# Last block of an attention and bilinear-GLU kernel: weight sums kept in DRAM, down products of two pairs at once, weight parts in a ring

## The chip, the cores and the metric

The kernel runs on one core of a Trainium2 chip. The metric is the device time in microseconds from the first to the last instruction of one execution. Three runs of the kernel before gave 2437.68, 2438.53 and 2443.07 us; the median is 2438.53 us. Engines are named as in the profile: PE is TensorE (PEld its weight loads), DVE VectorE, ACT ScalarE, POOL GpSimd, SP the engine that issues nearly all DMAs here.

## What is computed

The reference is a transformer block in float32 over 2048 rows of width 576. First comes attention with 32 query heads of 18 and one shared key and value head; then a bilinear GLU with 4608 hidden columns:

```python
h  = x + attention(layernorm(x))              # wq, wk, wv, wo
xn = layernorm(h)
h2 = h + ((xn @ w_gate) * (xn @ w_up)) @ w_down
```

The change touches only the second part, the products with w_gate, w_up and w_down.

## The kernel before

**Blocks and row blocks.** The 2048 rows are worked in four blocks of 512 (NB = 4, numbered 0 to 3). Hidden columns come in 36 groups of 128 (`f`); two neighbouring groups are a pair (NC = 18 pairs). Matmuls take float32 data in a faster 32-bit format, so that every operand is split into a high part (a copy, mostly on ACT) and a low part (operand minus high part, on DVE), and every product is made of three: high by high, high by low, low by high.

**Blocks 0 to 2** run in `ffn` (L905). Each step of the `f` loop, called a row block in the prediction, makes gate and up for 128 hidden columns with 27 double matmuls (L927, index `j` from 0 to 26 in the loop). In between stand the attention matmuls of later blocks (`pair`, L606 and L611, with their exponentials on ACT at L607), the split of the next weights (`split_w`, L808: high part on POOL at L92, low part on DVE at L93), and auxiliary work. After every second row block `down` (L843) makes the down product of the pair before.

**`down`** uses a seven-product scheme (Strassen-Winograd) on 2 x 2 blocks. The left operands are seven combinations of quarters of the hidden activations, in the tile `room` (A); the right operands are seven combinations of w_down, made at the start of the kernel and kept in DRAM (`wd_dram`), from which they come back through a ring of ten tiles (`wdo`, WD_BUFS = 10, `load_wd`). The product runs in 14 stages (`STAGES`, L1448): three matmuls of 128x288 into one of three PSUM banks, then an eviction which adds the bank to the residual `h`. Eight of the 14 evictions are one DVE instruction (L888); six are a copy on ACT (L892) and an add on POOL (L893).

**Block 3** runs in `last_block` (L1105). There attention is over, and gate and up too use the seven-product scheme, on quarters of the 512 input columns and rows. `ahead` (L977) prepares the activations during the last row blocks of block 2, a step at a time (the tables AHEAD and TURNS say at which `f` and `j`). The last 64 of the 576 input columns are added as a tail. For each pair, in this order, PE makes products 1, 2 (tail), 5, 6, 3 (tail), 7 (tail), 4 (tail), twelve matmuls of 128x256 each and four a tail (L1123, L1129). They go into two PSUM tiles: `s0`, whose two halves serve alternate pairs, and `s1`. Between products PE makes two, four or more stages of the down product of the pair before (`go`).

What follows a product, in each engine's own order of issue: copies of the PSUM banks to SBUF on ACT (c1, c5, c2), three adds on DVE (L1190 gu11, L1206 gu12, L1212 gu22), gate times up on POOL for three quarters of the hidden tile (`both_halves`, L1132: a11, a21, a22) and on DVE for the last (L1233 copies half of product 4's bank, L1234 multiplies: a12). The sums S of the quarters and their high and low parts (L92, L93) make the left operands A of the down product.

The weights of a pair are prepared while the pair before runs, in `prepare` (L1049): four loads of 256 KB and the tail weights, four POOL sums (L1074, L1081, L1087, L1093), seven high parts on ACT (L1058) and seven low parts on DVE (L1064), and both parts of the tail weights (L1060, L1066). Two full sets of seven weight tiles are held: one in freed tiles (`wrs`, `room`, `wps`, `wss`), one in the tile `XW`.

**Order.** The schedule is written out by hand: each engine works its instructions in the order in which the Python code issues them, and waits by semaphore for tiles that other engines write or free.

Of the kernel before, what the change touches and what calls it, by code (L numbers as in the profile page):

```python
# [26 lines left out]
P = 128  # L27
# [30 lines left out]
class Block:  # L58
# [846 lines left out]
    def ffn(self, b):  # L905
        pe, act, dve = self.pe, self.act, self.dve
        X, hid, todo = self.X, [], None
        ahead = self.ahead()
        for f in range(NF):
# [12 lines left out]
            for c in range(9):  # L922
                for wk, xk in ((0, 0), (0, 1), (1, 0)):
# [48 lines left out]
        self.load_wd(self.n_wd + 4)  # L972
# [4 lines left out]
    def ahead(self):  # L977
# [6 lines left out]
        for s in range(NQ):  # L984
            dve.tensor_scalar(xh[:, s, 0:D], h[:, s, :], mv[:, s, 0:1], rs[:, s:s + 1], ALU.subtract, ALU.mult)
            pool.tensor_copy(xh[:, s, D:], xh[:, s, 512:D])
            if s % 2:
                yield
# [10 lines left out]
        names = (1, 2, 5, 6, 3, 7, 4)  # L999
        self.XS = XS = {}  # L1000
        for i, k in enumerate(names[:5]):
            pl, tag = (self.pp, "P") if i < P_BUFS - 2 else (self.p2, "P2")
            XS[k] = pl.tile([P, 4, HT], F32R, tag=tag, name=f"XS{k}")
        XS[7], XS[4] = (self.kT[:, i * 4 * HT:(i + 1) * 4 * HT].rearrange("p (n q) -> p n q", n=4) for i in range(2))
        part = lambda i, j: raws[i][:, :, j * HT:(j + 1) * HT]
        sums = self.op.tile([P, 9, HT], F32, tag="ob", name="xsums")
        low = {k: sums[:, 2 * i:2 * i + 2] for i, k in enumerate((5, 6, 4, 7))}
        diff = sums[:, 8]
# [5 lines left out]
        dve.tensor_tensor(low[7], b22, b12, ALU.subtract)  # L1014
        yield
        src = {**low, 1: b11, 2: b21, 3: b22}
        for k in names:
            act.copy(XS[k][:, 0:2], src[k])
            dve.tensor_tensor(XS[k][:, 2:4], src[k], f32(XS[k][:, 0:2]), ALU.subtract)
            yield  # L1020
        xt = self.qp.tile([P, 4, HT], F32R, tag="q", name="XT_t")
        xd = self.qp.tile([P, 4, HT], F32R, tag="q", name="XT_d")
        rt = rt.rearrange("p (j q) -> p j q", j=2)
        act.copy(xt[:, 0:2], rt)
        dve.tensor_tensor(diff, rt[:, 0], rt[:, 1], ALU.subtract)
        dve.tensor_tensor(xt[:, 2:4], rt, f32(xt[:, 0:2]), ALU.subtract)
        act.copy(xd[:, 0], diff)
        dve.tensor_tensor(xd[:, 1], diff, f32(xd[:, 0]), ALU.subtract)
        self.Xt = [(xt[:, 0], xt[:, 2]), (xt[:, 1], xt[:, 3]), (xd[:, 0], xd[:, 1])]
        del rt, src, low, b11, b12, b21, b22, xt, xd, sums, diff, raws, part  # L1030
        yield
        raw = self.op.tile([P, 5, TB], F32, tag="ob", name="raw")
        self.raw = {k: raw[:, i] for k, i in ((1, 0), (6, 0), (2, 1), (3, 1), (5, 2), (4, 3), (7, 4))}
        self.wt_raw = self.wp.tile([P, 2, 2, P], F32, tag="wor", bufs=1, name="wt_raw")
        prep = self.prepare(0)
        next(prep)
        next(prep)
        yield
        sets = [self.wp.tile([P, 4 * HT], F32R, tag="wr", bufs=2, name=f"wrs{i}") for i in range(2)]
        sets += [self.o_hl.rearrange("p k q -> p (k q)")]  # L1040
        sets += [self.pp.tile([P, 4 * HT], F32R, tag="P", name=f"wps{i}") for i in range(2)]
        wss = self.wp.tile([P, 2, 4 * HT], F32R, tag="ws", bufs=2, name="wss")
        sets += [wss[:, 0], wss[:, 1]]
        as_set = lambda x: x.rearrange("p (l c g m) -> p l c g m", l=2, c=2, g=2)
        self.WS = [{k: as_set(x) for k, x in zip(names, sets)}, None]
        self.Wt = self.wp.tile([P, 2, 2, 2, P], F32R, tag="wos", bufs=1, name="wt")
        yield from prep

    def prepare(self, m):  # L1049

        act, dve, pool, sp = self.act, self.dve, self.nc.gpsimd, self.sp
        n = m % 2
        raw = self.raw
# [523 lines left out]
```

## Time and profile before

| | us |
|---|---|
| median of three runs | 2438.53 |
| the profiled execution's own time | 2437.47 |
| its span in the trace | 2435.7 |
| first row block of block 0 | from 377 |
| output of block 0 written from | 928 |
| output of block 1 written from | 1477 |
| first product of block 3 | 1963.3 |
| first product of pair 1 | 1992.6 |

The profiled execution's time is 1.8 us longer than its span. Busy shares of the span: PE 95%, PEld 68%, DVE 53%, ACT 63%, POOL 32%. The mean granted TensorE clock is 0.975 of full speed.

How to read the rows that the prediction shows: a row of the view by stage gives the window, its length, then for each engine the busy time and the number of instructions, the granted clock, the mean share of the DMA engines and their rate. A row of waits names who waited for whom, the total in us, how many times, and the longest. A row in order of time gives the start, the time from the first start to the last end, the engine and line, and in brackets the idle time ahead of it and what ended it; matmuls are pipelined, so that two rows overlap and their spacing is read from start to start. A row of groups gives the form, the count, busy us and mean ns of one, then the idle time ahead.

### The profile page before, as it was taken

The numbers are of one execution on the slowest core, as the hardware profiler recorded it, in microseconds if no ns is written. First come the engines' busy times: TensorE is split into PE (matmuls) and PEld (weight loads), VectorE is DVE, ScalarE is ACT, GpSimd is POOL, SyncE is SP. The second block draws the span as 40 slices with busy tenths as digits, with TensorE's granted clock in tenths as the row PEclk, the third lists the DMA queues.
The fourth block names the chain that finished last, engine by engine and source line by source line (L and its number), as shares of the span: only waits on it lengthen the run. The fifth ranks groups of instructions, "written<-read, shape, count | busy, mean of one in ns | idle before, by whom it ended". The sixth has DMA issues, their size and how long they took to land.

```text
span 2435.7 us, 46083 instructions
## 1 busy us (share of the span) xinstructions
PE 2304.3 (95%) x17958; PEld 1667.6 (68%) x17958; DVE 1291.1 (53%) x2238; ACT 1528.7 (63%) x2095; POOL 782.7 (32%) x892
## 2 busy tenths in 40 slices
PE   7999999999999999999999999999999987887887
PEld 5333346777777777777777777777777887877877
DVE  7556553434343454444444454444447677677675
ACT  6888877676767666676767675767662343344442
POOL 5345301222222222222222222222222355565563
PEclk9999999999999999999999999999999998888888
DMA  5788734333333336333333345334334444444442
GB/s 173 255 262 287 266 101 146 122 115 123 116 123 116 124 108 195 115 125 116 125 114 121 109 132 159 125 114 126 113 119 147 165 141 139 126 130 145 122 136 80
DMA packets 165428, 345.68 MB, mean 142 GB/s; under 512 B 17581, under 2 KB 49197, under 8 KB 165205
## 3 DMA queue, kind: packets, MB, share of 16 engines
q1 hardware_dynamic: 162469, 331.42, 42.7%
q0 software_dynamic: 2736, 11.26, 1.5%
q8 instruction: 143, 2.34, 0.4%
q14 instruction: 80, 0.66, 0.1%
HBM read 274.80 MB, written 55.67 MB: 136 GB/s over the span
## 4 chain that ended last, share of the span: by engine, by line
PE 71%; DVE 10%; ACT 3%; issue 3%; POOL 1%; DMA 1%; SPq 0%; DVEq 0%; ACTq 0%; POOLq 0%
PE pg L927 19%; PE acc L611 14%; PE y L882 14%; PE s L606 9%; PE pu L927 5%; PE gs L1123 5%; PE yo L736 2%; DVE XW L1064 2%; PE gu L927 1%; ACT room L92 1%; DVE h L888 1%; DVE room L93 1%; DVE wps L1064 1%; DVE S L1215 1%; PE y L855 1%
## 5 line engine op out<-in xcount | busy, mean ns | idle before, releaser
L607 ACT ACTIVATE P<-s 128x1024 f32<-128x1024 f32 x1024 | 1026.2, 1027 | 280.5 <-PE s L606 201.3
L927 PE MATMUL pu<-X,ws 64*128 64x512 f32 x2565 | 693.4, 389 | 0.0
L927 PE MATMUL pg<-X,ws 64*128 64x512 f32 x2565 | 692.9, 389 | 0.0
L893 POOL TENSOR_TENSOR h<-h,tmp 128x288 f32<-128x288 f32 x408 | 342.5, 863 | 802.5 <-ACT tmp L892 801.7
L927 PEld LDWEIGHTS pg<-X,ws 64*128 64x128 f32 x2565 | 475.3, 185 | 66.7 <-DMA wdo<-wd_dram 0.8
L611 PE MATMUL acc<-P,V 128*32 128x512 f32 x4096 | 490.2, 598 | 0.7 <-ACT P L607 0.6
L927 PEld LDWEIGHTS pu<-X,ws 64*128 64x128 f32 x2565 | 472.6, 185 | 16.4
L882 PE MATMUL y<-wdo,room 128*128 128x288 f32 x2856 | 429.3, 304 | 38.2 <-DVE h L888 38.2
L882 PEld LDWEIGHTS y<-wdo,room 128*128 128x128 f32 x2856 | 399.3, 193 | 84.1 <-DVE h L888 43.3
L606 PE MATMUL s<-q,kT 56*128 56x512 f32 x2048 | 437.9, 422 | 6.5 <-ACT P L607 3.9
L888 DVE TENSOR_TENSOR h<-h,y 128x288 f32<-128x288 f32 x544 | 235.1, 451 | 243.0 <-PE y L882 241.9
L892 ACT COPY tmp<-y 128x288 f32<-128x288 f32 x408 | 161.6, 402 | 302.3 <-PE y L882 298.6
L606 PEld LDWEIGHTS s<-q,kT 56*128 56x128 f32 x2048 | 196.8, 184 | 207.3 <-ACT P L607 120.4
L611 PEld LDWEIGHTS acc<-P,V 128*32 128x32 f32 x4096 | 114.4, 109 | 246.8 <-issue 234.5
L92 POOL CAST ws<-wr 128x1152 fp32r<-128x1152 f32 x108 | 126.6, 1173 | 382.2 <-PE pu L927 224.8
L955 DVE TENSOR_TENSOR hf<-pu,g 128x512 f32<-128x512 f32 x95 | 65.7, 692 | 340.9 <-ACT g L951 340.9
L93 DVE TENSOR_TENSOR ws<-wr,ws 128x1152 fp32r<-128x1152 f32 x108 | 148.9, 1379 | 60.8 <-POOL ws L92 60.8
L93 DVE TENSOR_TENSOR room<-S,room 128x1024 fp32r<-128x1024 f32 (+1 forms) x85 | 86.1, 1012 | 157.3 <-ACT room L92 156.8
L1123 PE MATMUL gs<-XS,XW 128*128 128x256 f32 x540 | 84.5, 313 | 33.6 <-DVE hfl L1234 33.2
L1123 PEld LDWEIGHTS gs<-XS,XW 128*128 128x128 f32 x540 | 77.9, 216 | 37.7 <-DVE hfl L1234 35.1
L92 ACT CAST room<-S 128x1024 fp32r<-128x1024 f32 (+1 forms) x85 | 74.0, 871 | 37.4 <-DVE S L1226 30.9
L1132 POOL TENSOR_TENSOR hfl<-gu 128x256 f32<-128x256 f32 x36 | 26.9, 747 | 185.8 <-DVE gu L1190 184.7
(241 smaller groups left out, 2454.5 us busy)
## 6 DMA issues: line engine op xcount, KB each, us to landing
wdo<-wd_dram SPq DMA_DIRECT2D x492, 288.0 KB
wr<-in_wgu_dram SPq DMA_DIRECT2D x108, 576.0 KB
wd_dram<-wd_room SPq DMA_DIRECT2D x20, 1008.0 KB
raw<-in_wgs_dram SPq DMA_DIRECT2D x72, 256.0 KB
q<-q_dram SPq DMA_DIRECT2D x64, 216.0 KB
q_dram<-qs SPq DMA_DIRECT2D x16, 504.0 KB
wd_dram<-wd_hi SPq DMA_DIRECT2D x7, 1008.0 KB
wd_dram<-wd_src SPq DMA_DIRECT2D x7, 1008.0 KB
```

The source lines that it names most:

```text
L92: (copy or self.cast)(hi, src)
L93: self.dve.tensor_tensor(lo, src, f32(hi), ALU.subtract)
L606: self.pe.matmul(s_[:, i], self.kT[o:o + 56, t * P:(t + 1) * P], q[o:o + 56, pr], start=True, stop=True)
L607: self.act.activation(p_, s_, AF.Exp, scale=SCALE)
L611: self.pe.matmul(acc[32 * j:32 * j + 32, :], self.V[:, t, :], Ps[j // 2][:, j % 2, :], start=(t == 0), stop=(t == NT - 1), skip_group_chec ...
L882: pe.matmul(y[:, :HD], m[:, t * P:(t + 1) * P], k, start=(first and j == 0), stop=(j == 2), skip_group_check=True)
L888: dve.tensor_tensor(hs, hs, y[:, :HD], ALU.add)
L892: act.copy(z, y[:, :HD])
L893: pool.tensor_tensor(hs, hs, z, ALU.add)
L927: pe.matmul(ps, w[o:o + 64, wk, c], X[o:o + 64, xk, c], start=(j == 0), stop=(j == 26))
L1064: dve.tensor_tensor(half(k, 1), raw[k], f32(half(k, 0)), ALU.subtract)
L1123: pe.matmul(bank[:, g * HT:(g + 1) * HT], W[:, wk, c, g], X[:, 2 * xk + c], start=(first and g == c == wk == xk == 0), stop=(c == 1 and wk ...
```

## The change

It has three parts.

1. **Weight sums in DRAM.** A new generator `weight_sums` makes the four sums of each of the 18 pairs on POOL during blocks 0 and 1, in two tiles that it takes from the `wdo` ring, and stores them in `wsum_dram`. One step (load, add, store) is taken at j = 8, 16 and 24 of each `f`. With two of the ten tiles held, the down weights are loaded eight ahead there (`load_wd(WD_BUFS - 2)`), and two more at the end of block 1.
2. **Down for two pairs.** In block 3, `down_pairs` makes the down product of pairs p - 2 and p - 1 together while pairs p and p + 1 run: 14 stages of six matmuls over four PSUM banks, three of each pair into the same bank, and one eviction for both. Four of the 14 evictions (ASIDE) go by ACT and POOL, ten by DVE. A has three copies in turn (AB), two of them in `XW`. Pair 16 goes alone behind the loop, then pair 17's plain products.
3. **Weight parts in a ring.** `prepare` goes. `feed(i)`, called behind each product i, makes the low part for product i + 2 (DVE), the high part for i + 3 (ACT) and the load for i + 7 (SP; of a plain weight for three products of seven, of a stored sum for four) in a ring of seven weight tiles and five raw ones.

Beside these the left operands' high and low parts are issued apart (`high`, `low`) instead of together, and `ahead` is cut into other steps with new tables.

```diff
+        if b == 0:
+            self.sums = self.weight_sums()
+            next(self.sums)
...
+                    if b < 2 and j in (8, 16, 24):
+                        next(self.sums, None)
...
-        self.load_wd(self.n_wd + 4)
+        self.load_wd(self.n_wd + (6 if b == 1 else 4))
...
+    def feed(self, i):
+        act, dve, sp = self.act, self.dve, self.sp
+        n = i + 2
+        if 0 <= n < 7 * NC:
+            w = self.WS[n % 7]
+            dve.tensor_tensor(w[:, 1], self.raw[:, n % 5], f32(w[:, 0]), ALU.subtract)
+        n = i + 3
+        if 0 <= n < 7 * NC:
+            act.copy(self.WS[n % 7][:, 0], self.raw[:, n % 5])
+        n = i + LEAD
+        if 0 <= n < 7 * NC:
+            m, k = divmod(n, 7)
+            sp.dma_start(self.raw[:, n % 5], self.wgs[m, :, (0, 1, None, None, None, None, 2)[k]] if k in (0, 1, 6) else self.wsum_dram[m, :, k - 2])
...
+    def weight_sums(self):
+        pool, sp = self.nc.gpsimd, self.sp
+        u, v = (self.wp.tile([P, TB], F32, tag="wdo", bufs=WD_BUFS, name=f"wsum{i}") for i in range(2))
+        for m in range(NC):
+            for k, (loads, to, x, y, op) in enumerate((([(u, 3), (v, 2)], u, u, v, ALU.add), ([(v, 0)], u, u, v, ALU.subtract),
+                                                       ([(v, 1)], v, v, u, ALU.subtract), ([(u, 0), (v, 3)], u, u, v, ALU.subtract))):
+                for t, j in loads:
+                    sp.dma_start(t, self.wgs[m, :, j])
+                yield
+                pool.tensor_tensor(to, x, y, op)
+                yield
+                sp.dma_start(self.wsum_dram[m, :, k], to)
+                yield
+
+    def down_pairs(self, b, pairs):
+        banks = [self.ps_f(f"yq{pairs[0]}_0"), self.ps_f(f"yq{pairs[0]}_1"), self.ps_m(f"yq{pairs[0]}_2"), self.ps_a(f"yq{pairs[0]}_3")]
+        for i, (bank, (x, w), first, (s, n)) in enumerate(QUAD):
+            W = [self.wdo.pop((b, p, w)) for p in pairs]
+            for t in range(2):
+                y = banks[2 * bank + t]
+                for z, (p, v) in enumerate(zip(pairs, W)):
+                    A = self.AB[(p + 1) % 3]
+                    for j, (k, l) in enumerate(((0, 0), (0, 1), (1, 0))):
+                        pe.matmul(y[:, :HD], A[:, k, x, t * P:(t + 1) * P], v[:, l], start=(first and z == j == 0),
...
+                if 2 * i + t not in ASIDE:
+                    dve.tensor_tensor(hs, hs, y[:, :HD], ALU.add)
+                else:
...
+                    act.copy(z, y[:, :HD])
+                    pool.tensor_tensor(hs, hs, z, ALU.add)
+                if t:
+                    del W, v
+                    self.load_wd(self.n_wd + len(pairs))
+                yield
```

The new order behind product 7 of a pair (`i + 5`), up to the next pair's product 1:

```diff
+            product(i + 5, a)
+            tail(1, 1, a)
+            dve.tensor_tensor(gu22, a, c5, ALU.add)
+            both_halves(a22, gu22)
...
+                dve.tensor_tensor(S[:, 2], a11, a21, ALU.subtract)
+                high(5, S[:, 2])
+            go(2)
...
+            self.feed(i + 5)
+
+            product(i + 6, a)
+            tail(1, 2, a)
...
+                low(5, S[:, 2])
                 dve.tensor_tensor(S[:, 0], a21, a22, ALU.add)
+                high(2, a22)
                 dve.tensor_tensor(S[:, 1], S[:, 0], a11, ALU.subtract)
+                go()
+                high(3, S[:, 0:2], 2)
+                low(2, a22)
             g = self.hh.tile([P, TB], F32, tag="g", bufs=1, name=f"gl{p}")
             act.copy(g[:, 0:HT], a[:, 0:HT])
+            if not end:
+                low(3, S[:, 0:2], 2)
             dve.tensor_tensor(a12, a[:, HT:], g[:, 0:HT], ALU.mult)
```

In the changed file gu22 is L1207, S[:, 2] L1213, the DVE eviction L1108, the weight low part L1058, the left operands' low part L1157, S[:, 0] and S[:, 1] L1230 and L1232, a12 L1240.

More of the change, by code (lines that the diff above doesn't have):

```diff
@@ L1029, in ahead @@
+        for i in range(len(todo) + 1):
+            if i < len(todo):
+                act.copy(todo[i][0], todo[i][2])
+            if i:
+                hi, lo, x = todo[i - 1]
+                dve.tensor_tensor(lo, x, f32(hi), ALU.subtract)
+            yield
         self.Xt = [(xt[:, 0], xt[:, 2]), (xt[:, 1], xt[:, 3]), (xd[:, 0], xd[:, 1])]
[L1030 to L1032 removed]
@@ L1033, in ahead @@
-        self.raw = {k: raw[:, i] for k, i in ((1, 0), (6, 0), (2, 1), (3, 1), (5, 2), (4, 3), (7, 4))}
+        del rt, src, low, b11, b12, b21, b22, xt, xd, sums, diff, raws, part, todo, hi, lo, x
+        self.raw = self.op.tile([P, 5, TB], F32, tag="ob", name="raw")
         self.wt_raw = self.wp.tile([P, 2, 2, P], F32, tag="wor", bufs=1, name="wt_raw")
[L1035 to L1039, printed above, removed]
```

294 lines of the change are left out of this document (126 added, 168 removed).

## The prediction

> **What bounds the kernel now.** I read the page's slices first, then busy time by stage, PE's waits, PE's order of time inside the last block, and the granted clock in short windows.
>
> ```profile
> span 2435.7 us, 46083 instructions
> PE   7999999999999999999999999999999987887887
> DVE  7556553434343454444444454444447677677675
> PEclk9999999999999999999999999999999998888888
> 930.00:1476.00 546.00, 545.24 (x4499) 394.51 (x4496) 252.97 (x453) 373.55 (x482) 128.87 (x151) 1.00 0.40 127
> 1600.00:1963.00 363.00, 354.09 (x2866) 270.39 (x2864) 194.93 (x358) 198.31 (x288) 102.40 (x120) 0.99 0.41 130
> 1992.60:2436.00 443.40, 355.57 (x2462) 342.56 (x2462) 302.10 (x492) 175.56 (x384) 241.12 (x217) 0.87 0.42 128
> ```
>
> The stage rows give PE, PEld, DVE, ACT, POOL, granted clock, DMA share, GB/s. Up to 1963 us (blocks 0 to 2) PE is hardly idle and its clock is full: 0.8 us of 546 are free in block 1, 9 of 363 at the end of block 2. In the last block (1963 to 2436) PE loads weights 342.6 us of 443.4 and the clock falls to 0.87. Only there is time to be won.
>
> ```profile
> PE gs L1123 <- DVE hfl L1234: 55.1, 17, 4.0
> PE y L882 <- DVE h L888: 30.4, 18, 1.9
> 2412.60 1.59 PE L1123 MATMUL gs<-XS,XW 128*128 128x256 f32 x12
> 2414.03 0.95 PE L882 MATMUL y<-wdo,room 128*128 128x288 f32 x6
> 2414.82 1.60 PE L1123 MATMUL gs<-XS,XW 128*128 128x256 f32 x12
> 2416.26 0.64 PE L1129 MATMUL gs<-XT_t,wt 128*128 128x256 f32 x4
> 2416.74 0.95 PE L882 MATMUL y<-wdo,room 128*128 128x288 f32 x6
> 2424.62 0.64 PE L1129 MATMUL gs<-XT_d,wt 128*128 128x256 f32 x4
> 2431.00 0.65 PE L1156 MATMUL gs<-wdo,room 128*128 128x288 f32 x3 [0.55 <-DVE h L1170]
> 1932.77 5.94 PE L882 MATMUL y<-wdo,room 128*128 128x288 f32 x33 [3.50 <-DVE h L888]
> 1963.33 1.70 PE L1123 MATMUL gs<-XS,wrs 128*128 128x256 f32 x12
> 1968.67 0.53 PE L855 MATMUL y<-wdo,room 128*128 128x288 f32 x2 [3.25 <-ACT room L92]
> 1992.60 0.62 PE L1123 MATMUL gs<-XS,XW 128*128 128x256 f32 x3 [3.99 <-DVE hfl L1234]
> ```
>
> Two waits carry it: product 1 of the next pair waits for DVE's product at L1234 (both lie in the tile s0; 3.24 us a pair), and a stage of the down product waits until DVE has emptied its bank (30.4/17 = 1.8). The last pair, with no weights to prepare, shows undisturbed PE by start-to-start times: 12 matmuls of a product 1.43 us, six of a down stage 0.79, a tail of four 0.48. A pair is 7 x 1.43 + 4 x 0.48 + 42/6 x 0.79 = **17.46 us** of PE. It takes (2425.1 - 1992.6)/17 = 25.4. PEld is idle 443.4 - 342.6 = 100.8 us, about 6 of it behind the last matmuls, so 5.6 a pair; the remaining 2.4 is the lowered clock. The fault is DVE's queue, 302.1/17 = 17.8 us of work a pair in an order that PE waits for.
>
> **The clock**, in windows as long as its own steps:
>
> ```profile
> 2215.50:2218.91 3.41, 1.59 (x12) 1.36 (x12) 2.98 (x7) 1.02 (x3) 3.41 (x4) 1.00 0.54 172
> 2218.91:2222.32 3.41, 2.56 (x13) 2.27 (x11) 3.18 (x6) 1.61 (x4) 1.54 (x2) 0.50 0.67 200
> 2222.32:2225.74 3.42, 1.71 (x8) 1.71 (x9) 2.98 (x6) 1.42 (x4) 0.00 (x0) 0.50 0.82 258
> 2242.80:2246.22 3.42, 2.32 (x19) 2.32 (x19) 3.02 (x6) 1.45 (x3) 3.42 (x4) 1.00 0.54 177
> 2246.22:2249.63 3.41, 0.24 (x2) 0.03 (x1) 2.81 (x5) 1.10 (x2) 0.32 (x1) 1.00 0.86 250
> 2249.63:2253.04 3.41, 2.91 (x13) 2.91 (x14) 2.32 (x6) 0.81 (x2) 0.00 (x0) 0.50 0.52 198
> 2253.04:2256.46 3.42, 3.42 (x29) 3.34 (x27) 1.39 (x3) 0.74 (x2) 0.00 (x0) 1.00 0.32 86
> 2010.70:2014.11 3.41, 1.77 (x14) 1.67 (x14) 3.02 (x7) 0.91 (x2) 3.41 (x4) 1.00 0.44 164
> 2014.11:2017.52 3.41, 0.89 (x8) 0.68 (x6) 2.82 (x6) 1.61 (x4) 0.96 (x1) 1.00 0.81 250
> ```
>
> The clock changes at the ends of fixed 3.41 us windows. After 1.36 us of weight loads in a window it halves; after 1.67 or 2.32 it does not. At half it returns after 2.91, not after 2.27. So an idle stretch of some 1.9 us inside one window costs a window at half clock, about 1.65 us of matmuls.
>
> **The change, part by part**, with these rows:
>
> ```profile
> L1064 DVE TENSOR_TENSOR XW<-raw,XW 128x512 fp32r<-128x512 f32 x57 | 60.1, 1076 | 0.2
> L93 DVE TENSOR_TENSOR room<-hf,room 128x512 fp32r<-128x512 f32 x19 | 13.0, 685 | 0.7 <-ACT room L92 0.7
> L888 DVE TENSOR_TENSOR h<-h,y 128x288 f32<-128x288 f32 x136 | 59.1, 448 | 39.1 <-PE y L882 38.3
> L1212 DVE TENSOR_TENSOR gu<-gs,cs 128x512 f32<-128x512 f32 x17 | 11.5, 678 | 1.4 <-PE gs L1129 1.4
> L1066 DVE TENSOR_TENSOR wt<-wt_raw,wt 64x512 fp32r<-64x512 f32 x16 | 11.7, 732 | 10.6 <-ACT wt L1060 10.6
> L93 DVE TENSOR_TENSOR room<-S,room 128x256 fp32r<-128x256 f32 x17 | 7.2, 425 | 0.6
> L1234 DVE TENSOR_TENSOR hfl<-gs,gl 128x256 f32<-128x256 f32 x18 | 7.5, 418 | 3.1 <-ACT gl L1233 3.1
> L1087 POOL TENSOR_TENSOR raw<-raw 128x512 f32<-128x512 f32 x16 | 27.9, 1741 | 0.0
> L1074 POOL TENSOR_TENSOR raw<-raw 128x512 f32<-128x512 f32 x16 | 20.7, 1292 | 0.0
> L1132 POOL TENSOR_TENSOR hfl<-gu 128x256 f32<-128x256 f32 x34 | 25.2, 741 | 183.4 <-DVE gu L1190 182.3 <-DVE gu L1212 1.1
> DMA packets 30276, 59.63 MB, mean 126 GB/s; under 512 B 3360, under 2 KB 3360, under 8 KB 30240
> GB/s 173 255 262 287 266 101 146 122 115 123 116 123 116 124 108 195 115 125 116 125 114 121 109 132 159 125 114 126 113 119 147 165 141 139 126 130 145 122 136 80
> ```
>
> *Sums moved.* 72 POOL adds of 1.29 to 1.74 us leave block 3 for blocks 0 and 1, with 108 loads and 72 stores of 256 KB on SP's queue. The steps stand a third of a row block apart (546/36/3 = 5.1 us): load, add, store. Cover: POOL works 129 us of 546 there, DVE 253, and no add stands ahead of the weight cast of the same row block. An add that waits for its load holds POOL's eviction adds and the next weight cast, and through that DVE; a load that waits for the store before it holds SP's loads of down weights, queries and heads. All of these are wanted several us later. Between 0 (nothing is removed there, so no gain) and 72 x 1.74 = 125 us I take 2, nearer PE's 0.8 us of idle time. The down ring keeps eight places of ten; seven are wanted every second row block, 30 us: nothing.
>
> *Weight parts in block 3.* Seven low parts a pair stay on DVE, at 1.08 us beside POOL's sums, 0.69 without them (the 685 ns row of the same size): -2.7 us a pair. Three more loads a pair: 15 transfers are 7 x 288 + 8 x 256 KB = 4.2 MB, at 21.4 us 195 GB/s against a mean of 126 now and 287 in the page's fourth slice: nothing, while each raw load has four products (9 us) to land.
>
> *Down for two pairs.* 14 evictions for 28: DVE's five a pair instead of eight (-1.3 us), POOL's two for six. A stage is six matmuls over four banks, so the 1.8 us bank wait goes. DVE a pair: 7 x 0.69 + 0.73 + 3 x 0.68 + 5 x 0.45 + 9 x 0.43 + 0.69 + 0.42 = 14.8 us, below PE's 17.46.
>
> *What is late next* is the same L1234 product (L1240 in the new file): the instruction order shows that the next product 1 still waits for it. Count from the end of product 7's tail. PE: two stages to 1.58, product 4 and its tail to 3.49, one stage to 4.28. DVE in its queue's order: 0.1 hand-over, 0.68 (L1207), 0.42 (L1213), 0.45 (L1108), a weight low 0.69, the tail's low 0.73, 0.43, 0.42, 0.42, eight gaps of 0.02: 4.5; then the last stage's eviction 0.45, lows 0.43 and 0.69, L1240 0.42, gaps: 6.6. PE idles 6.6 - 4.28 = 2.3 us. In odd pairs DVE's early eviction is that of the second stage, ready at 1.78: 0.5 later, 2.8. I take **2.6**; bounds are 0.2 (L1234 straight behind the tail, less a stage) and today's 3.24. Another 0.1 is for product 5 behind gu11 (0.79 of stage against 0.1 + 0.69).
>
> *Clock.* A 2.6 us gap leaves 1.9 in one window about two times in three; 0.64 x 1.65, and a second window now and then: **1.2 us** a pair (bounds 0 and 2.4).
>
> Period: 17.46 + 2.6 + 0.1 + 1.2 = **21.36 us**.
>
> *The rest of the block.* Pair 0, 29.3 us now (1963.3 to 1992.6): only two lows and three highs are made ahead, so ACT is free sooner; the 3.25 us start wait falls to about 1.2, the end wait to 2.6, clock 1.2: 22.5. Pair 1 has one down stage: 7 x 1.43 + 1.92 + 0.79, waits of 0.85 twice, 2.8 and 1.3 of clock: 18.5. Pairs 2 to 16: 15 x 21.36 = 320.4. Pair 17 up to its last tail: 16.8. Behind it 10.6 us now (2425.1 to 2435.7); afterwards a stage 0.8, pair 16's 14 half stages alone 5.6 and some 1.3 of bank waits, eight last groups 6.3, then, as now behind the last matmul (2431.65 to 2435.7), some 4.2 of eviction and store: 18.2. The 3.5 us wait in row block 32 loses perhaps 2, as fewer steps run ahead there; that cancels the 2 above.
>
> Sum: 22.5 + 18.5 + 320.4 + 16.8 + 18.2 = 396.4 against 2435.7 - 1963.3 = 472.4: **-76**. The profiled execution took 2437.5 (span 2435.7), so 2361.5; the median of the runs, 2438.5, is 1 us above it: **2362**.
>
> **Rivals.** *A, the chain stays long*: gap 3.24 and clock 2.4, as now, 23.2 us a pair: +28, with pairs 0 and 1 **2393**. For it: POOL's eviction adds and DVE's two-input operations still meet, 1.08 against 0.69 us where they do now. *B, the clock stays full*: -1.2 x 17: **2342**, and with a 1.5 us gap 2327. The row at 2215.50 speaks against it; that at 2010.70, with 1.77 busy and no drop, for it. The Trainium skill (TensorE: Matmul & The Clock Gate, "Why this matters for your kernels") warns only of PE gaps above some 3 us; by that no gap here lowers the clock. The trace disagrees: its gaps of about 1.8 us in the window at 2215.50 did.
>
> *C, slower*: the moved sums reach PE's path in blocks 0 and 1. POOL and DVE hold each other up (the 1.74 against 1.29 us rows), and DVE frees the banks of a PE with no idle time. All 72 in full give 2362 + 125 = **2487**; it ends above before by over 0.2% from 1.13 us each. The Trainium skill (SBUF — State Buffer, "Who interferes with whom") speaks against the change here: a DVE instruction with two SBUF inputs and a GpSimd one that reads SBUF lock each other out for a whole instruction. Block 3's rows agree; whether it reaches PE in blocks 0 and 1 no run here shows yet. *D, the change doesn't do what it says*: loads come late, and each pair waits for DMA. At 150 GB/s 4.2 MB take 28 us: +6.4 x 15 gives **2458**.
>
> **How the numbers follow.** My forecast (2343 to 2380) has 0.47, B 0.20, A and what lies up to 2425 0.23, no change 0.02, C 0.05, D 0.03. A measurement of this kernel tells some 0.2% (5 us) from no change. Faster 0.90, same 0.02, slower 0.08. The range takes in A's and B's times and leaves out the upper tail of A, the slower cases and a little below B: 2322 to 2404.
>
> **What would show it.** Blocks 0 to 2 as long as now within 5 us and PE idle there under 2; the wait of y for DVE gone; product 1 still waiting for L1240, 17 times, at 2.3 to 2.8 us; weight lows at 0.7 to 0.8; the clock in block 3 at 0.92 to 0.95; a period near 21.4; the end 8 us longer. Wrong if block 1 lengthens by over 10 us, if the period is below 20 or above 23, or if PE waits for raw or wsum loads.

## The result, and the profile after

The changed kernel takes **2357.48 us** (median of four runs, 2355.46 to 2357.93) where the kernel before takes 2438.70 on the same chip (four runs, 2437.68 to 2443.07): a ratio of **0.9662**, 95% interval 0.9645 to 0.9679. The profiled execution took 2357.88 us, its span is 2356.1. The forecast was 2362 us.

The page of the changed kernel, first its span and slices (the same rows as those of the kernel before):

```profile
span 2356.1 us, 46348 instructions
PE   7999999999999999999999999999999999888888
DVE  7565644444444455445454555444444766667665
PEclk9999999999999999999999999999999999999999
```

The fall of the clock to eight tenths in the last slices is gone. Busy time by stage (PE, PEld, DVE, ACT, POOL, clock, DMA share, GB/s); the last row is block 3 from the first product of pair 1:

```profile
1600.00:1965.60 365.60, 359.48 (x2926) 275.92 (x2922) 195.39 (x361) 204.17 (x293) 99.22 (x117) 1.00 0.41 133
930.00:1476.00 546.00, 543.01 (x4476) 397.80 (x4473) 274.63 (x449) 373.12 (x479) 180.40 (x185) 1.00 0.52 169
1986.70:2356.10 369.40, 322.07 (x2468) 312.20 (x2468) 243.92 (x467) 159.48 (x340) 79.45 (x88) 0.98 0.59 190
```

Blocks 0 to 2 end 2.3 us later than before (1965.6 against 1963.3). Block 3 takes 390.5 us instead of 472.4: the whole gain is there. From pair 1 on, PEld is idle for 57 us where it was idle for 101, DVE has 244 us of work instead of 302, POOL 79 instead of 241, and the clock is 0.98 instead of 0.87.

PE's waits in block 3 of the changed kernel:

```profile
PE gs L1138 <- DVE hfl L1240: 40.7, 17, 2.9
PE gs L1262 <- DVE h L1266: 1.2, 2, 0.6
PE yq L1104 <- DVE h L1108: 0.9, 1, 0.9
```

Product 1 still waits for a12, 2.39 us a pair instead of 3.24. The wait of a down stage for its bank, 30.4 us before, is down to one of 0.9. DVE's groups in block 3 (2006 to 2310 us):

```profile
L1108 DVE TENSOR_TENSOR h<-h,yq 128x288 f32<-128x288 f32 x73 | 33.0, 452 | 61.0 <-PE yq L1104 61.0
L1058 DVE TENSOR_TENSOR wrs<-raw,wrs 128x512 fp32r<-128x512 f32 x29 | 24.9, 857 | 0.0
L1058 DVE TENSOR_TENSOR wps<-raw,wps 128x512 fp32r<-128x512 f32 x30 | 20.5, 682 | 0.0
...
L1074 DVE TENSOR_TENSOR wt<-wt_raw,wt 64x512 fp32r<-64x512 f32 x14 | 13.6, 968 | 0.4
```

Most weight low parts have fallen from 1.08 to 0.68 us. Those that meet a POOL instruction in the chain have not. The wrs part in the chain takes 0.87 or 1.22 us by turns (the wrs row's mean of 0.86 takes in a second wrs part, outside the chain, at 0.68); the tail's takes 1.25 or 0.69, where the kernel before had a mean of 0.73. The chain from product 7's tail to the next product 1, on DVE and then on PE, at one boundary:

```profile
2105.91 0.69 DVE L1207 TENSOR_TENSOR gu<-gs,cs 128x512 f32<-128x512 f32 x1 [0.54 <-PE gs L1145]
...
2107.21 0.87 DVE L1058 TENSOR_TENSOR wrs<-raw,wrs 128x512 fp32r<-128x512 f32 x1
2108.11 1.25 DVE L1074 TENSOR_TENSOR wt<-wt_raw,wt 64x512 fp32r<-64x512 f32 x1
...
2111.90 0.42 DVE L1240 TENSOR_TENSOR hfl<-gs,gl 128x256 f32<-128x256 f32 x1
```

```profile
2105.70 0.56 PE L1104 MATMUL yq<-wdo,XW 128*128 128x288 f32 x3
...
2112.37 0.84 PE L1138 MATMUL gs<-XS,wrs 128*128 128x256 f32 x3 [2.16 <-DVE hfl L1240]
```

From the end of product 7's tail (2105.70, where the next stage starts) to product 1 are 6.7 us; the forecast counted 6.6. The gaps alternate between 2.15 and 2.63; the forecast was 2.3 and 2.8. Start to start, pair 2 to pair 17:

```profile
2005.49 0.74 PE L1138 MATMUL gs<-XS,wrs 128*128 128x256 f32 x4 [2.94 <-DVE hfl L1240]
...
2134.64 0.63 PE L1138 MATMUL gs<-XS,wrs 128*128 128x256 f32 x3 [2.63 <-DVE hfl L1240]
...
2175.64 0.63 PE L1138 MATMUL gs<-XS,wrs 128*128 128x256 f32 x3 [2.63 <-DVE hfl L1240]
...
2318.87 0.86 PE L1138 MATMUL gs<-XS,wrs 128*128 128x256 f32 x5 [2.16 <-DVE hfl L1240]
```

(2318.87 - 2005.49)/15 = 20.89 us a pair; the forecast was 21.36. Two pairs at full clock take 2175.64 - 2134.64 = 41.0, so 20.5 each; the remaining 0.4 a pair is lost to the clock.

### The profile page after: what moved, and what is told of

It reads as the page before. It is cut to its first block, busy times and chain, and to the rows that moved or that the text cites. A ratio compares the mean times of both kernels' runs of the same rounds, so it can differ in the third digit from the quotient of the medians.

```text
span 2356.1 us, 46348 instructions
## 1 busy us (share of the span) xinstructions
PE 2270.4 (96%) x17958; PEld 1644.1 (70%) x17958; DVE 1269.4 (54%) x2209; ACT 1509.7 (64%) x2046; POOL 714.0 (30%) x826
## 4 chain that ended last, share of the span: by engine, by line
PE 77%; DVE 7%; DMA 1%; ACT 1%; issue 1%; SPq 0%; POOL 0%; DVEq 0%; ACTq 0%
PE pg L930 21%; PE acc L611 15%; PE y L882 13%; PE s L606 9%; PE gs L1138 7%; PE pu L930 3%; PE yq L1104 3%; PE yo L736 3%; PE gu L930 2%; PE gs L1145 1%; DVE XW L1157 1%; DVE wt L1074 1%; DVE wrs L1058 1%; ACT P L607 0%; DMA raw<-wsum_dram 0%
## 5 line engine op out<-in xcount | busy, mean ns | idle before, releaser
L893 POOL TENSOR_TENSOR h<-h,tmp 128x288 f32<-128x288 f32 x306 | 238.6, 809 | 603.2 <-ACT tmp L892 602.0
L882 PEld LDWEIGHTS y<-wdo,room 128*128 128x128 f32 x2142 | 291.1, 189 | 46.4 <-issue 34.8
L882 PE MATMUL y<-wdo,room 128*128 128x288 f32 x2142 | 304.6, 301 | 5.0 <-DVE h L888 5.0
L888 DVE TENSOR_TENSOR h<-h,y 128x288 f32<-128x288 f32 x408 | 176.5, 452 | 198.8 <-PE y L882 198.7
L892 ACT COPY tmp<-y 128x288 f32<-128x288 f32 x306 | 122.3, 400 | 241.7 <-PE y L882 225.0
L1087 POOL TENSOR_TENSOR wsum<-wsum,wsum 128x512 f32<-128x512 f32 x72 | 98.1, 1363 | 174.1 <-DMA wsum<-in_wgs_dram 174.1
L93 DVE TENSOR_TENSOR room<-S,room 128x1024 fp32r<-128x1024 f32 x51 | 62.8, 1231 | 135.3 <-ACT room L92 135.3
L1138 PE MATMUL gs<-XS,wrs 128*128 128x256 f32 x432 | 63.5, 299 | 40.7 <-DVE hfl L1240 40.7
L1138 PEld LDWEIGHTS gs<-XS,wrs 128*128 128x128 f32 x432 | 58.2, 202 | 45.4 <-DVE hfl L1240 45.0
L1104 PE MATMUL yq<-wdo,XW 128*128 128x288 f32 x504 | 87.4, 302 | 1.0 <-DVE h L1108 0.9
```

The lines of the kernel that those rows point to most:

```text
L93: self.dve.tensor_tensor(lo, src, f32(hi), ALU.subtract)
L882: pe.matmul(y[:, :HD], m[:, t * P:(t + 1) * P], k, start=(first and j == 0), stop=(j == 2), skip_group_check=True)
L888: dve.tensor_tensor(hs, hs, y[:, :HD], ALU.add)
L892: act.copy(z, y[:, :HD])
L893: pool.tensor_tensor(hs, hs, z, ALU.add)
L1104: pe.matmul(y[:, :HD], A[:, k, x, t * P:(t + 1) * P], v[:, l], start=(first and z == j == 0), stop=(z == len(pairs) - 1 and j == 2), skip_ ...
```

## The experiments

The theory at this point: DVE's queue between gu22 and a12 sets the gap, POOL's sums had lengthened its instructions, and each long gap costs clock beside its own length. Twelve kernels test it. Runs of different chips are compared by their ratio to the kernel before on the same chip. Times are medians.

### What the moved sums cost in blocks 0 and 1

```diff
-            self.sums = self.weight_sums()
...
-                        next(self.sums, None)
...
-            sp.dma_start(self.raw[:, n % 5], self.wgs[m, :, (0, 1, None, None, None, None, 2)[k]] if k in (0, 1, 6) else self.wsum_dram[m, :, k - 2])
+            sp.dma_start(self.raw[:, n % 5], self.wgs[m, :, k % 4])
```

> This kernel makes no weight sums in blocks 0 and 1 and loads a plain weight where the changed kernel loads a stored sum (72 POOL adds, 108 loads and 72 stores are left out, so that four products of seven work on wrong weights); block 3 is issued as in the changed kernel. My theory: the moved sums cost PE 2 us in blocks 0 and 1; the first product of block 3 starts at 1963 to 1964 us where the changed kernel starts it at 1965.6, and the time is 2353 to 2357 us against 2357.5. Rival C (the sums reach PE's path): the start falls by 10 us or more, and the time ends under 2348. A second rival, that the sums cost nothing and the 2.3 us come from the new steps of ahead: the start stays at 1965.6.

2356.58 us (2351.96 to 2357.37), ratio 0.9649 (0.9636 to 0.9663) against 0.9662: the difference is too small for the runs. The traces tell it. DVE's weight low parts in block 1 (930 to 1476 us) before and after, the sums in the page of the changed kernel, and then its PE's waits in blocks 0 and 1:

```profile
L93 DVE TENSOR_TENSOR ws<-wr,ws 128x1152 fp32r<-128x1152 f32 x36 | 50.6, 1406 | 24.6 <-POOL ws L92 24.6
L93 DVE TENSOR_TENSOR ws<-wr,ws 128x1152 fp32r<-128x1152 f32 x36 | 66.1, 1835 | 24.6 <-POOL ws L92 24.6
L1087 POOL TENSOR_TENSOR wsum<-wsum,wsum 128x512 f32<-128x512 f32 x72 | 98.1, 1363 | 174.1 <-DMA wsum<-in_wgs_dram 174.1
```

```profile
PE y L855 <- ACT room L92: 1.3, 1, 1.3
PE yo L736 <- DVE h L737: 1.1, 1, 1.1
```

The sums slow DVE's weight low parts there from 1.41 to 1.84 us, and it reaches PE hardly anywhere: these two waits are 1.1 and 0.9 us longer than without the sums. From the first row block of block 0 to the output of block 1 are 1099.9 us in the kernel before and 1100.1 without sums; with them 1103.5 (from 378.79 to 1482.28), and 1102.7 to 1103.7 in the ten later kernels here that have them. So the sums cost **3 us**; the forecast was 2. Against that the stretch from there to block 3 became 2 to 3 us shorter (486.4 before, 483.3 in the changed kernel, 484.5 in this one). The expected start of block 3 was missed (1965.6 again) because this execution was 2.2 us later than the changed kernel's at the first row block (380.97 against 378.79), where the kernels here scatter from 376.6 to 381.0 whatever their edit. The price of rival C, 1.13 us and more each, is excluded: 3 us over 72 adds is 0.04 each.

### The sums alone, in the kernel before

```diff
-        pool.tensor_tensor(raw[7], raw[1], raw[5], ALU.subtract)
...
-        pool.tensor_tensor(raw[5], raw[5], raw[4], ALU.add)
...
-                act.copy(half(k, 0), raw[k])
+                act.copy(half(k, 0), raw[{7: 5, 6: 5, 3: 2}.get(k, k)])
...
```

> The kernel before, without the four POOL sums a pair in block 3 (left out: four products of seven work on plain weights), everything else as it was: down for one pair at a time, two sets of weight tiles, the old order. It measures the first part of the change alone, free of its cost in blocks 0 and 1. If POOL's sums lengthened DVE's chain: weight lows fall from 1.08 towards 0.7 us, the wait of product 1 from 3.24 by about 1 us, the clock rises above 0.87, and the time falls by 20 to 45 us (2393 to 2418). Rival, the long chain is DVE's own count of instructions: within 6 us of 2438. If the sums were all of the gain: 2365 or less.

**2380.34 us** (2379.69 to 2381.69), ratio 0.9753 (0.9736 to 0.9769): 60 us, more than expected. PE's waits in block 3:

```profile
PE gs L1119 <- DVE hfl L1230: 49.0, 17, 3.5
PE y L882 <- DVE h L888: 6.4, 17, 0.5
```

The bank wait, 1.8 us a pair before, falls to 0.38 with the sums gone, though there are still 14 evictions for each pair and three banks. Product 1's wait falls from 3.24 to 2.88, and the clock (2006 to 2280 us) rises to 0.96. 1.41 + 0.36 us of waits a pair is half of 60/17 = 3.5; the other half is clock. So the bank wait came mostly of POOL's sums, and not of the number of stages and evictions. The edit frees two things at once: DVE's instructions that the sums held up (low parts of the XW weights fall from 1.08 to 0.85 us) and ACT's high parts that waited for the sums; this run doesn't separate them.

### POOL's load given back, in three places

Four idle POOL adds of 128x512 a pair in the changed kernel. First (e2) they are issued with four of a pair's seven weight steps, in `feed`:

```diff
+            if n % 7 in (2, 3, 4, 5):
+                self.nc.gpsimd.tensor_tensor(V, self.raw[:, n % 5], self.raw[:, n % 5], ALU.add)
```

Then all four stand behind a11 (e7, shown), or in the same way behind `both_halves(a22, gu22)` (e8); V stands for `self.V.rearrange(...)`, a tile that is no longer read.

```diff
             both_halves(a11, gu11)
+            for _ in range(4):
+                pool.tensor_tensor(V, V, V, ALU.add)
```

> The changed kernel with four more POOL adds of 128x512 a pair in block 3, which write a tile nobody reads (nothing is left out). It gives POOL about the load that the sums were there before the change (four adds of 1.3 to 1.7 us, some 6 us a pair), and leaves DVE's and PE's instructions alone. Theory 1, POOL and DVE hold each other up and DVE's chain is what PE waits for: weight lows go from 0.69 towards 1.0 us, the wait of product 1 for L1240 grows from 2.4 by 0.5 to 1.5 us, and the time by 10 to 25 us (2367 to 2382). Rival, what left POOL was off the path: the lows and the wait stay within 0.1 us and the time within 4 us of 2357.5.

> The changed kernel with four idle POOL adds of 128x512 a pair, all behind a11 (nothing is left out): as many as in the kernel with more POOL load, where two of the four ran beside DVE's chain between gu22 and a12. If the place decides, the chain is untouched: the wait of product 1 stays at 2.3 to 2.7 us and the time within 2355 to 2368. If POOL's load as such decides (DVE's whole work grows), the time is 2395 to 2415 as there.

> The same four idle POOL adds a pair, all behind a22 (nothing is left out), so that POOL is busy through the whole chain from gu22 to a12. If the place decides: each of the chain's DVE instructions with both inputs in SBUF grows by 0.4 to 0.7 us, some five of them, the wait of product 1 goes to 4 to 5.5 us, the clock halves once or twice a pair, and the time is 2415 to 2460. If POOL's load as such decides: as with the four adds elsewhere, 2395 to 2415, or 2357 if it costs nothing.

e2 takes **2409.41 us** (2408.49 to 2412.14, ratio 0.9875), e7 **2375.46** (2372.54 to 2379.62, 0.9733), e8 **2430.76** (2428.72 to 2433.37, 0.9951). By the ratios, against the changed kernel's 0.9662 of 2438.7 us, the same work costs 52, 17 and 70 us by its place. PE's wait for a12, of e2, e7 and e8 in this order:

```profile
PE gs L1140 <- DVE hfl L1242: 65.9, 17, 4.4
```

```profile
PE gs L1138 <- DVE hfl L1242: 41.0, 17, 2.9
```

```profile
PE gs L1138 <- DVE hfl L1242: 86.5, 17, 6.0
```

In e7 the wait is that of the changed kernel (40.7), in e2 it is 3.88 us a pair, in e8 5.09. How that comes about is seen in e2's trace, POOL's first two adds at one boundary, and then DVE's instructions beside them:

```profile
2099.78 2.94 POOL L1063 TENSOR_TENSOR V<-raw 128x512 f32<-128x512 f32 x2
```

```profile
2099.17 1.20 DVE L1058 TENSOR_TENSOR wrs<-raw,wrs 128x512 fp32r<-128x512 f32 x1
2100.40 1.42 DVE L1076 TENSOR_TENSOR wt<-wt_raw,wt 64x512 fp32r<-64x512 f32 x1
2101.85 1.15 DVE L1159 TENSOR_TENSOR room<-S,room 128x256 fp32r<-128x256 f32 x1
2102.93 0.41 DVE L1232 TENSOR_TENSOR S<-hfl,hfl 128x256 f32<-128x256 f32 x1
```

Three DVE instructions of 0.69, 0.69 and 0.43 us take 1.20, 1.42 and 1.15; the next, behind them, takes 0.41 again. The first meets POOL's eviction add (2099.02 to 2099.83), as in the changed kernel; the other two meet the new adds. Two of e2's four adds lie in the chain. My estimate of 10 to 25 us for e2 was too low: it took the gap for the whole price. The gap grew by 1.49 us a pair, which is 25 us; the clock fell from 0.98 to 0.89, which is as much again (52/17 = 3.05 a pair). In e7 the place outside the chain was not quite free either: weight low parts there take 1.10 instead of 0.68, PE's weight loads wait 0.3 us a pair for one of them (PEld, 15 times, 4.5 us), and the longer pair halves the clock more often (0.95; see the last experiment). That expectation was missed by 7 us; e8's wait and time came out as expected.

### Down for one pair at a time

```diff
-            for _ in range(n):
+            for _ in range(2 * n):
                 next(D, None)
...
-            if p % 2 == 0 and p:
+            if p:
                 drain(D)
-                D = self.down_pairs(b, (p - 2, p - 1))
+                D = self.down_pairs(b, (p - 1,))
...
```

> The changed kernel with the down product of one pair at a time: 14 stages of three matmuls while the next pair runs, two stages where there was one, over the same four banks; ten evictions a pair on DVE instead of five, eight instructions on ACT and POOL instead of four (nothing is left out; pair 16's stages run inside pair 17, so the end is 6 us shorter). My theory: DVE has two more evictions (0.9 us) ahead of L1240 in the chain, and a stage again finds its bank full, some 0.4 us twice; the wait of product 1 goes from 2.4 to 3 or 3.4 us, the clock halves more often, period 22 to 23.3; time 2363 to 2386 us. Rival, pairing saved nothing that was on the path: period 21.3 as now and only the shorter end is seen, 2350 to 2354 us.

**2395.95 us** (2393.66 to 2396.87), ratio 0.9810 (0.9794 to 0.9827): by the ratios 36 us slower than the changed kernel, and 10 us above the upper end expected. PE's waits:

```profile
PE gs L1138 <- DVE hfl L1240: 44.1, 17, 2.9
PE yq L1104 <- ACT tmp L1112: 17.0, 16, 1.1
```

The chain grew little (2.59 a pair). What is new is 1.06 us a pair of a stage that waits for a bank which ACT empties, and the clock falls to 0.94. So pairing does remove a bank wait in the new order, one for ACT, which I had not priced.

By the ratios the sums alone bring 60 us in the kernel before (e11, without their cost of 3), the change without pairing 46 (e5), the whole change 82. So the ring and the new order without pairing bring nothing beyond the sums but cost some 11 us (more, as e5's end is also shorter), and pairing brings 36 on top. No kernel here has pairing without the ring, so that what the ring is worth by itself is not shown.

### Product 1 away from a12's tile, and weight parts earlier

The first edit alone is e3; with the second, in `feed`, it is e4.

```diff
-            a, b_, c = s0[:, p % 2], s1[:, 0], s1[:, 1]
+            t0, t1 = (s0, s1) if p % 2 == 0 else (s1, s0)
+            a, b_, c = t0[:, 0], t1[:, 0], t1[:, 1]
```

```diff
-        n = i + 2
+        n = i + 3
...
-        n = i + 3
+        n = i + 4
...
-LEAD = 7
+LEAD = 8
```

> The changed kernel with the two PSUM tiles exchanged in every second pair: product 1 of a pair goes to the tile which product 7 and 4 of the pair before did not use, so that it no longer waits for L1240 (nothing is left out). Theory 1, the wait only moves: product 1 starts at once, and product 2 comes 1.43 us later and finds its own weight low part, which stands in DVE's queue behind a12 and the lows of the left operands, not yet made; some 1 to 1.8 us of idle PE a pair in place of 2.4. Period 20 to 20.9, time 2337 to 2352 us. Theory 2, the wait for the tile is all there is: the gap falls under 0.4, the period to 17.7 to 18.5, the time under 2315. Theory 3, DVE's queue as a whole is full and sets the period: time within 4 us of 2357.5.

> As the kernel with exchanged PSUM tiles, and with the weight parts made one product earlier (low part for product i + 3, high for i + 4, load for i + 8; nothing is left out). If product 1's wait for a12 and then product 2's for its weight low part are the two waits behind each other, both go: period 17.7 to 18.8, full clock in block 3, time 2305 to 2325 us. If DVE's work itself were the bound (14.8 us a pair by the durations alone, a little more with contention), period above 19.5 and PE waiting for DVE at other places: 2335 to 2357 us.

e3 takes 2350.99 us (2349.66 to 2353.10, ratio 0.9633), e4 **2321.08** (2319.71 to 2325.62, ratio 0.9517). PE's waits in e3:

```profile
PE gs L1138 <- DVE wrs L1058: 24.7, 17, 1.5
PE gs L1138 <- DVE hfl L1241: 3.5, 8, 0.7
```

and in e4:

```profile
PE gs L1138 <- DVE gu L1183: 9.5, 17, 1.0
PE gs L1138 <- DVE hfl L1241: 3.6, 8, 0.8
```

As theory 1 had it, in e3 the wait only moves to product 2, which lacks its weight low part (1.45 us a pair). Of 2.39 us 0.7 were won, and by the ratios only 7 us of time: the 1.45 us gap follows the 0.40 us gap of every second pair 0.5 us later, and the clock is 0.96. With the parts made one product earlier the wait for the weight low part goes too, 0.2 us a pair is left of the wait for a12, and the clock is 1.00 (2006 to 2280 us). DVE's work is the same; the shared tile and the order of DVE's queue were the bound.

### What is left: gu11, and a wait on ACT

All three start from e4. The first edit is e6, the second e9; e10 has both, and the third, by which the parts of a12 and S[:, 3] are issued behind the next pair's copy of product 1's bank.

```diff
-            a, b_, c = t0[:, 0], t1[:, 0], t1[:, 1]
+            a, b_, c = t0[:, 0], t1[:, 0], t0[:, 1]
```

```diff
-            self.feed(i)
-
             product(i + 1, c, True)
...
             both_halves(a11, gu11)
+            self.feed(i)
```

```diff
             act.copy(c1, a)
+            for f in late:
+                f()
...
-                high(1, a12)
-                high(6, S[:, 3])
-                low(1, a12)
-                low(6, S[:, 3])
+                late = [lambda A_=A, x=a12: (high(1, x, 1, A_), high(6, S[:, 3], 1, A_), low(1, x, 1, A_), low(6, S[:, 3], 1, A_))]
```

> The kernel with exchanged tiles and early weight parts, with product 2 moved to the other half of the tile of product 1, so that product 5 no longer waits for gu11 and product 2 no longer for a12 (nothing is left out). If those two waits (0.56 and 0.2 us a pair there) are what is left, the period goes from 18.76 to 18.0 to 18.2 and the time from 2321 to 2307 to 2312 us. Rival: product 2 now waits for the copy of product 1's bank on ACT, and product 6 for gu11, 0.5 us or more together: 2317 to 2327 us.

> The kernel with exchanged tiles and early weight parts, with gu11 ahead of the weight parts of the same step in DVE's queue (nothing is left out). There product 5 waits 0.56 us a pair for gu11, which found DVE still at work on what stood ahead of it. If the order of DVE's queue is the cause: the wait falls to 0.1 to 0.2, the period from 18.76 to 18.2 to 18.4, the time from 2321 to 2311 to 2316 us. Rival, DVE is behind in its work there whatever the order: the wait moves to a weight low part or stays, 2319 to 2324 us.

> The kernel in which product 2 had moved to the other half of product 1's tile (2348 us, product 2 waited 2.07 us a pair for the copy of product 1's bank, which stood on ACT behind two high parts that wait for a12), with those high parts and their low parts issued behind that copy, and with gu11 ahead of the weight parts (nothing is left out). If only the order in ACT's queue is the cause: the wait for the copy goes under 0.2 us, no wait for gu11 or a12 is left, period 17.8 to 18.2, full clock, 2303 to 2311 us. Rival, the late left operands now hold up a down stage, or product 6 waits for gu11: 2317 us or more.

e6 takes 2348.46 us (2348.03 to 2349.14, ratio 0.9617), slower than either expected. PE's wait, and ACT's queue at one boundary:

```profile
PE gs L1138 <- ACT cs L1177: 35.2, 17, 2.6
```

```profile
2043.36 0.41 ACT L1154 CAST XW<-hfl 128x256 fp32r<-128x256 f32 x1 [0.87 <-DVE hfl L1241]
2043.77 0.41 ACT L1154 CAST XW<-S 128x256 fp32r<-128x256 f32 x1
2044.11 0.62 ACT L1061 CAST wps<-raw 128x512 fp32r<-128x512 f32 x1
2044.63 0.58 ACT L1177 COPY cs<-gs 128x512 f32<-128x512 f32 x1
```

The rival was right, and its price was four times what I gave it. Product 2 waits for the copy of product 1's bank, and that copy stands on ACT behind two high parts that wait for a12: the old chain, by way of another engine's queue (2.07 us a pair). With these high parts behind the copy, e10 takes **2310.05 us** (2309.57 to 2313.24, ratio 0.9469, interval 0.9453 to 0.9485):

```profile
PE gs L1138 <- ACT cs L1176: 6.3, 11, 1.5
```

The wait for the copy, 0.37 us a pair, stayed above the 0.2 expected, and the period is 18.26 us where 17.8 to 18.2 were expected. In ACT's order of time a weight high part still stands ahead of the copy (at 2072.96 and 2073.49); that it is the rest of the wait was not tested. e9, which is e4 with gu11 moved ahead in DVE's queue, takes **2312.21** (ratio 0.9474; one of its four executions took 9323 us, of which there is no trace, the others 2311.4 to 2312.7); its wait for gu11 is gone. Both are 5.3% faster than the kernel before and 2% faster than the changed kernel.

### Why the clock stayed higher than forecast

```diff
             tail(0, 0, c)
+            tail(0, 0, c)
```

> The changed kernel with the four tail matmuls behind product 2 issued twice (that part of gate is counted twice): 0.48 us more PE work a pair far from the wait of product 1, which should stay at 2.15 and 2.63 us. It tests why the clock in block 3 was 0.98 and not 0.92 to 0.95. In the changed kernel two pairs at full clock take 41.0 us, and twelve of the clock's windows of 3.413 us take 40.96, so that each gap falls on the same place of a window as two pairs before; from 2134 us on that place is an edge between two windows, and no gap halves the clock. Theory 1, this fit is the reason: with 41.96 us for two pairs the gaps drift by a third of a window every two pairs, and four to twelve of the pairs 2 to 16 run a window at half clock (two to three in the changed kernel): 17 x 0.48 = 8 us of matmuls and 3 to 13 of clock, 2368 to 2379 us, clock 0.93 to 0.97 in block 3. Rival, gaps of this length seldom halve the clock whatever their place: as many halvings as now, 2364 to 2367 us and 0.98.

2373.58 us (2369.92 to 2375.53, ratio 0.9731, interval 0.9714 to 0.9747). The gaps are unchanged (17 of them, 40.8 us), the clock is 0.96 from 2006 to 2320 us. Read by the spacing of the first products, 6 of the 15 pairs from 2 to 16 lost a stretch at half clock (10.4 us together) where the changed kernel has 4 (6.1 us). By the ratios it is 17 us above the changed kernel, by the two spans 14. 8.2 are the matmuls themselves; of the rest the profiled executions show 4.3 us of clock in pairs 2 to 16 and 1.4 from pair 17 on. That is theory 1, at the lower end of its count, and 7 us above the rival, with one profiled execution of each kernel. That the changed kernel had two or three such pairs was wrong: it has four. Windows of the changed kernel around the boundary shown above and around the next:

```profile
2109.18:2112.59 3.41, 1.25 (x9) 1.00 (x8) 3.31 (x9) 1.13 (x3) 0.00 (x0) 1.00 0.51 179
2112.59:2116.00 3.41, 3.41 (x17) 3.41 (x17) 1.64 (x4) 1.86 (x5) 0.00 (x0) 0.50 0.17 56
2129.66:2133.07 3.41, 2.35 (x19) 2.10 (x18) 3.31 (x7) 0.79 (x3) 0.70 (x1) 1.00 0.83 237
2133.07:2136.48 3.41, 1.84 (x15) 1.84 (x16) 3.31 (x8) 2.12 (x6) 0.00 (x0) 1.00 0.60 199
2136.48:2139.90 3.42, 3.39 (x28) 3.13 (x27) 1.88 (x5) 1.06 (x3) 0.00 (x0) 1.00 0.39 133
```

The first gap, 2.16 us, lies in one window: 1.25 us of matmuls there, and the next window runs at half clock. That window at half clock delays everything behind it by about 1.5 us, and so the next gap, 2.63 us and longer, falls across an edge: 2.35 and 1.84 us of matmuls in the two windows, and the clock stays. From then on two pairs take 41.0 us and twelve windows 40.96, so that every later gap falls on an edge again, to the end of the block.

The kernel before shows the same hold at a lowered clock. Every second product 1 there starts 51.20 to 51.24 us after the last (2096.47, 2147.71, 2198.93, 2250.13), which is 15 windows (51.20), and the stretches at half clock return at that distance (from 2116.51, 2167.71 and 2218.91, three windows each). Its clock of 0.87 was thus no matter of chance from pair to pair either.

## Why the prediction was right, and where its terms were not

**The sum.** 390.5 us for block 3 against a forecast of 396.4, and 2.3 us later at its start against 0. By parts: pair 0 21.1 (forecast 22.5), pair 1 18.8 (18.5), pairs 2 to 16 313.4 (320.4), pair 17 17.1 (16.8), the end 20.1 (18.2; the eight last groups take 8.2 for 6.3, with two waits for their evictions). That the total lies within 5 us is in part luck: over pairs 2 to 16 the clock is 12 us and the gap 3 us below its term, and small waits are 8 us above theirs.

**Sums in blocks 0 and 1, 2 us:** 3 us. Right in place and nearly in size; POOL and DVE hold each other up there too (1.41 to 1.84 us), and little of it reaches PE. The sign "PE idle there under 2" failed by a little: 3.0 us of 546 in block 1, 0.8 before. Of the 2.3 us at the start of block 3, 1.8 lie ahead of the first row block (378.79 against 376.95), within that scatter. The loss of the 3.5 us wait in row block 32, 2 us, was wrong in its place, since that wait is still 3.2; but the other three of these waits fell from 4.2 to 1.8 us together.

**Weight low parts at 0.69:** right for most (0.68). The forecast held all of the chain's instructions to be undisturbed. Two are not (0.87 and 1.25 us at the boundary shown, 0.7 more than forecast). But DVE instructions start on average 0.05 us before the one ahead ends, where the forecast had gaps of 0.02, and over the eleven starts that makes up for it.

**"A stage is six matmuls over four banks, so the 1.8 us bank wait goes":** the wait went, but the step gave the wrong reason. With the sums alone taken out, 1.4 of the 1.8 us go. Pairing was needed against another wait, for ACT (1.06 us in the kernel without it).

**The gap, 2.6 us:** 2.39, at the place and with the alternation that was forecast (2.15 and 2.63 against 2.3 and 2.8). The experiments show that it is set by the tile that product 1 shares with a12 and by the order of DVE's queue, and not by the amount of DVE's work: with the same work, another tile and another order it vanishes (e3 and e4).

**Product 5 behind gu11, 0.1 us:** 0.2, and the forecast has no term for other small waits. A pair at full clock takes 20.5 us, 0.64 more than 17.46 + 2.39. Start to start, the stage ahead of product 5 takes 0.2 us too long, products 1 and 5, which stand behind a wait, 0.1 each, and the hand-over to product 1 0.2.

**The clock, 1.2 us a pair:** 0.41. This is the largest error in a term (12 us over 15 pairs), and the error in the small waits hid two thirds of it. The price of one loss, 1.65 us, was near (1.5). The step that failed took each gap's place in a window for chance, two in three for a loss. But a loss moves the next gap, and a period that fits the windows holds it: 4 pairs of 15 lost. The clock, forecast at 0.92 to 0.95, was 0.98.

**The rivals.** A (the long chain) did not come; the kernels with POOL's load given back show that it would have, with the sums still beside the chain. B (full clock, 2342) was nearest on the other side: the clock is nearly full, but not because such gaps leave it alone. The gap of 2.16 us within one window at 2109.18 does halve it, so that the Trainium skill's rule in TensorE: Matmul & The Clock Gate ("Why this matters for your kernels"), by which only gaps above some 3 us matter, fails in this trace too. C is excluded by the kernel without sums. The rule in SBUF — State Buffer ("Who interferes with whom") that was weighed for it agrees with the traces here as to the lock-out (0.43 us to 1.15 beside POOL's adds in e2, an eviction 0.45); whether that costs time is decided by what waits for the instruction held up, 0.04 us an add in blocks 0 and 1, up to 70/68 = 1.0 us, clock included, in the chain of block 3 (e8). D did not come: from pair 1 on DMA moves 190 GB/s, and PE waits for no load.

## What to carry to other kernels

Price an instruction of a second engine by whose queue it runs beside: the same four POOL adds cost 17, 52 or 70 us, by whether DVE instructions that PE waits for ran at that moment. When a wait is removed, walk every in-order queue that the released engine depends on next; where the wait only moved to another result of DVE (e3) the edit brought 7 us, and with a new order of that queue 35 (e4); where it moved to ACT (e6) 24 of these 35 were lost, and with a new order there, and e9's edit, it is 47 (e10). And a gap on PE costs its length and, if it leaves too little work in one clock window (here under some 1.6 us of 3.41), some 1.5 us more, so that near the limit a few tenths of a microsecond decide over several times as much.

## What the runs showed of the hardware

A window of 3.41 us with 1.25 us of matmuls was followed by one at half clock, one with 1.84 was not (2112.59 and 2136.48 above); both had one gap, of 2.16 and 2.63 us. The longer gap cost less, because of its place. Over all windows at full clock from pair 0 to pair 17 in the 14 traces, every one with at most 1.55 us of matmuls was followed by one at half clock, and none with 1.67 or more; in between both occur. A program whose period is near a whole number of windows (41.0 against 40.96 us for twelve) can so keep a full clock over ten gaps in a row, and lose it with 0.48 us more work a pair.

A DVE instruction with both inputs in SBUF that meets a POOL add of 128x512 was held up for up to 0.73 us, to between two and three times its length (0.69 to 1.42, 0.43 to 1.15). POOL is held up too: the idle adds of e2 take 1.04 us at the shortest and 1.50 at the longest. In e2 they take turns: POOL from 2099.78 to 2101.27, DVE from 2100.40 to 2101.82, POOL from 2101.35 to 2102.72, DVE from 2101.85 to 2103.00; each ends at most its own undisturbed length after the end of the other. An eviction, which reads a PSUM bank, was not: the one at 2106.85 of the changed kernel takes 0.45 us beside a POOL instruction from 2106.74 to 2107.53, and evictions that overlap a POOL instruction by more than 0.3 us take 0.44 to 0.46 us in block 3 of every kernel here.
